# Fused attention and MLP block on one core: the second score matmul of a slot moved in between the value matmuls

## The chip, the cores and the metric

One core of a Trainium2 chip. The metric is the time on the device in microseconds (us). The kernel before takes 1401.2 us (median of 3 runs, 1400.7 to 1401.65).

Names in the profile: PE is TensorE's matmuls, PEld its weight loads, ACT is ScalarE, DVE VectorE, POOL GpSimd. `f_S` is the score buffer in PSUM, `f_PQ` holds q and the exponentials, `f_KV` holds K and V, `f_O` the attention output in PSUM, `f_M` the PSUM buffer of the projections.

## The reference

```python
def _A_ref(x, k_cache, v_cache, wq, wo):             # x 1x2048x640, 32 heads, 2048 keys, head size 128
    q = (x @ wq)...                                  # heads split off
    scores = einsum('bhqd,bhkd->bhqk', q, k_cache) * Dh ** -0.5
    p = _softmax(scores); o = einsum('bhqk,bhkd->bhqd', p, v_cache)
    return o... @ wo
# around it: modulation from c, layernorm, residual; then _B_ref: layernorm, GELU, shifts, w2, layernorm, w3, GELU, w4
```

All in bf16. About 1190 of the 1400 us are attention, the rest is the MLP part (called the tail here).

## The kernel before

The program lists operations with priorities; a planner then fixes each engine's order. On PE the order is simply by priority. Attention runs in 128 steps (8 groups of 4 heads x 4 chunks of 512 queries x the head in the group), each of 8 slots, one per pair of key tiles. In a slot PE computes two 512-column score matmuls into one of two score buffers (`S0`, `S1`, used in turn), and ACT takes the exponential of the whole buffer, 128x1024. The value matmuls of a key tile (four of 129 columns: two for each of two output buffers) follow about three slots later. Query projection (`q_proj`) and output projection (`wo_group`) fill in.

```python
S_ps = [ps("S%d" % i, [128, 1024]) for i in range(2)]        # the two score buffers
PV_SLOTS = [2, 2, 3, 2, 2, 3, 2]                             # key tiles' value matmuls per slot
...
for j in range(NP):                                          # NP = 8 slots in step s
    n = s * NP + j
    sp = Tile(pool="S%d" % (n % 2))
    pt = PT[n % NPT]
    for r in range(2):
        kt = 2 * j + r
        P.op("PE", lambda e, ...: e.matmul(sp[:, r * QC:(r + 1) * QC], K_ap[b][:, kt * 128:(kt + 1) * 128], q.ap, start=True, stop=True),
             MM(QC), (K[b][kt // 4], q), (sp,), n + 0.01 * r, accum=True)            # last number: priority
    x = P.op("ACT", lambda e, ...: e.activation(pt.ap..., sp.ap, ACT.Exp, scale=SCALE), 1021, (sp,), (pt,), n)
    for r in range(2):
        u = 2 * j + r
        ...                                                  # slot, acc from PV_SLOTS
        key = NP * s + 3 + slot + 0.3 + 0.01 * (u - acc)
        for bk in range(2):
            kb = key + 0.004 * bk if u < NKT - 2 else NP * s + 9.35 + 0.02 * bk + 0.001 * u
            P.op("PE", pv, 2 * MM(129), (pt, V[b]), (o[bk],), kb, accum=True)        # pv: two matmuls
# q_proj of the next step: priority NP * s + 2.3 + ...; output projection: about n + 0.6
```

Two facts follow from the code. A slot's first score matmul can't start before the exp of two slots earlier has read the buffer. And that exp can't start before the second score matmul of its own slot is done.

## Time and profile before

The page of the profiled run. After the bar of a group line come busy time, mean ns of one instruction, then the idle time of the engine before the group and what ended it.

```profile
span 1395.0 us, 29964 instructions
...
PE 1380.7 (99%) x13176; PEld 939.8 (67%) x13176; DVE 518.0 (37%) x1337; ACT 1114.6 (80%) x1195; POOL 123.5 (9%) x106
...
PE 96%; ACT 2%; POOL 1%; DVE 0%; DMA 0%; issue 0%; ACTq 0%; POOLq 0%
...
L714 ACT ACTIVATE f_PQ<-f_S 128x1024 bf16<-128x1024 f32 x1024 | 1030.2, 1023 | 155.0 <-PE f_S L712 147.6
...
L731 PE MATMUL f_O<-f_KV,f_PQ 128*128 128x129 bf16 x8192 | 612.2, 220 | 0.2 <-ACT f_PQ L714 0.2
L712 PE MATMUL f_S<-f_PQ,f_KV 128*128 128x512 bf16 x2048 | 608.9, 379 | 3.1 <-ACT f_PQ L714 2.7
```

PE is nearly the whole chain of waits; exp waits for scores (147.6 us in all), scores hardly for exp (2.7 us). But 99% busy doesn't say how near to its limit PE is, since matmuls overlap in the records. That is read from the starts. One slot in the PE timeline (columns: start us, us, engine, line, operation, tiles, count):

```profile
701.80 0.59 PE L712 MATMUL f_S<-f_PQ,f_KV 128*128 128x512 bf16 x2
702.23 0.62 PE L731 MATMUL f_O<-f_KV,f_PQ 128*128 128x129 bf16 x8
702.68 0.30 PE L668 MATMUL f_M<-f_wo,f_OO 128*128 128x320 bf16 x1
702.82 0.59 PE L712 MATMUL f_S<-f_PQ,f_KV 128*128 128x512 bf16 x2
```

Two scores take 0.43 us, eight value matmuls 0.45 us (56 ns each), one output projection 0.14 us: a slot of 1.02 us. Taken one by one, the start-to-start gaps are 216 ns for 512 columns, 136 for 320: each is the columns divided by 2.4 GHz plus about 2.5 ns. I call that the floor. From the first to the last score matmul, everything above it sums to 9.28 us; in steps 9 to 118, to 4.59 us of some 1026 us (42 ns a step).

Then the slack. This is the timeline ahead of a slot with twelve value matmuls (slot 5), ACT, PEld and PE together:

```profile
699.13 2.05 ACT L714 ACTIVATE f_PQ<-f_S 128x1024 bf16<-128x1024 f32 x2 [0.73 <-PE f_S L712]
...
700.41 0.23 PEld L712 LDWEIGHTS f_S<-f_PQ,f_KV 128*128 128x128 bf16 x2
700.55 0.38 PE L712 MATMUL f_S<-f_PQ,f_KV 128*128 128x512 bf16 x1
```

The first of the two exps ends at 699.13 + 1.02 = 700.15; the score matmul that reuses its buffer starts at 700.55, about 0.39 us later, and its weight load at 700.41. The exp is done in good time. Slots are counted from 0; slots 0 and 5, both with twelve value matmuls, have the least slack (388 ns by the median of steps 9 to 119), since the two slots ahead of each are the shortest pairs, 1.02 us each.

### The profile page before, as it was taken

Reading aid. Unit: us, or ns where it says so; the run is one execution under the profiler, and the core shown is the slowest. Engines: PE = TensorE matmul, PEld = TensorE weight load, DVE = VectorE, ACT = ScalarE, POOL = GpSimd, SP = SyncE. Lnnn points to the kernel's source line nnn. Section 1 sums busy time; section 2 is a strip of 40 time slices with the busy share of each in tenths; the row PEclk is TensorE's granted clock in tenths of the full one; section 3 lists DMA queues with packets and bytes.
Section 4 is the critical chain, followed back from the end, with each engine's and each line's share of the span. In section 5 each row is a group of like instructions: output and inputs, shape, how many; then the busy total and the mean of one; then the engine's idle time right before and its main releaser. Section 6 shows DMA issues by size and latency. Waiting matters only on the chain.

```text
span 1395.0 us, 29964 instructions
## 1 busy us (share of the span) xinstructions
PE 1380.7 (99%) x13176; PEld 939.8 (67%) x13176; DVE 518.0 (37%) x1337; ACT 1114.6 (80%) x1195; POOL 123.5 (9%) x106
## 2 busy tenths in 40 slices
PE   8999999999999999999999999999999999899998
PEld 6666676766676667666776677666766766555554
DVE  4453333233323332333223332333233345595552
ACT  5988888888888888888888888888888888864222
POOL 0000000000000000000000000001233376600000
PEclk9999999999999999999999999999999999999999
DMA  9551623261214221241215112612254112411110
GB/s 203 126 110 34 134 61 85 51 107 35 47 35 88 55 47 35 55 88 33 49 22 98 33 40 33 107 35 47 54 103 102 17 31 55 111 39 48 34 39 24
DMA packets 258963, 88.82 MB, mean 64 GB/s; under 512 B 236625, under 2 KB 257554, under 8 KB 258834
## 3 DMA queue, kind: packets, MB, share of 16 engines
q1 hardware_dynamic: 256210, 85.41, 30.1%
q8 instruction: 104, 1.70, 0.5%
q10 hardware_dynamic: 2624, 1.51, 0.5%
q14 instruction: 25, 0.20, 0.1%
HBM read 43.48 MB, written 2.62 MB: 33 GB/s over the span
## 4 chain that ended last, share of the span: by engine, by line
PE 96%; ACT 2%; POOL 1%; DVE 0%; DMA 0%; issue 0%; ACTq 0%; POOLq 0%
PE f_O L731 33%; PE f_S L712 31%; PE f_M L643 10%; PE f_M L668 10%; PE f_S L890 2%; PE f_M L890 2%; PE f_S L877 2%; PE f_O L877 2%; ACT f_PQ L836 1%; PE f_S L413 1%; PE f_S L850 1%; PE f_M L850 1%; POOL f_y L511 0%; PE f_S L832 0%; PE f_M L623 0%; DMA f_xin<-in_A_x_dram 0%
## 5 line engine op out<-in xcount | busy, mean ns | idle before, releaser
L714 ACT ACTIVATE f_PQ<-f_S 128x1024 bf16<-128x1024 f32 x1024 | 1030.2, 1023 | 155.0 <-PE f_S L712 147.6
L731 PEld LDWEIGHTS f_O<-f_KV,f_PQ 128*128 128x128 bf16 x8192 | 539.6, 98 | 211.4 <-ACT f_PQ L714 0.4
L731 PE MATMUL f_O<-f_KV,f_PQ 128*128 128x129 bf16 x8192 | 612.2, 220 | 0.2 <-ACT f_PQ L714 0.2
L712 PE MATMUL f_S<-f_PQ,f_KV 128*128 128x512 bf16 x2048 | 608.9, 379 | 3.1 <-ACT f_PQ L714 2.7
L676 DVE TENSOR_TENSOR f_y<-f_M,f_y 128x320 f32<-128x320 f32 x192 | 94.4, 492 | 524.8 <-PE f_M L668 524.8
L668 PE MATMUL f_M<-f_wo,f_OO 128*128 128x320 bf16 x992 | 270.2, 299 | 0.0
L712 PEld LDWEIGHTS f_S<-f_PQ,f_KV 128*128 128x128 bf16 x2048 | 192.0, 98 | 46.6 <-ACT f_PQ L714 3.9
L643 PE MATMUL f_M<-f_hT,f_wq 128*128 128x512 bf16 x640 | 159.2, 379 | 0.1
L511 POOL TENSOR_TENSOR f_y<-f_y,f_mod 128x640 f32<-128x640 f32 x40 | 61.3, 1542 | 1058.2 <-DVE f_y L676 1050.8
L668 PEld LDWEIGHTS f_M<-f_wo,f_OO 128*128 128x128 bf16 x992 | 94.9, 97 | 27.9
L643 PEld LDWEIGHTS f_M<-f_hT,f_wq 128*128 128x128 bf16 x640 | 62.4, 98 | 75.9 <-DVE f_hT L557 0.9
L740 DVE TENSOR_TENSOR f_OO<-f_O,f_rl 128x256 bf16<-128x256 f32 x256 | 108.4, 423 | 8.3
L646 DVE CAST f_PQ<-f_M 128x512 bf16<-128x512 f32 x128 | 88.5, 691 | 54.8 <-PE f_M L643 54.7
L738 DVE RECIPROCAL f_rl<-f_O 128x2 f32<-128x2 f32 x256 | 43.5, 170 | 45.9 <-PE f_O L731 41.7
L880 ACT ACTIVATE f_OO<-f_O 128x512 bf16<-128x512 f32 (+1 forms) x28 | 16.7, 596 | 33.2 <-PE f_O L877 33.1
L880 ACT ACTIVATE f_OO<-f_S 128x512 bf16<-128x512 f32 (+1 forms) x28 | 16.6, 595 | 30.7 <-PE f_S L877 30.7
L674 DVE COPY f_y<-f_M 128x320 f32<-128x320 f32 x32 | 15.7, 490 | 67.5 <-PE f_M L668 67.5
L890 PE MATMUL f_S<-f_KV,f_OO 128*128 128x320 bf16 x224 | 34.3, 300 | 0.0
L890 PE MATMUL f_M<-f_KV,f_OO 128*128 128x320 bf16 x224 | 34.3, 300 | 0.0
L472 DVE BATCH_NORM_STATS2 f_small<-f_y 128x6 f32<-128x320 f32 x64 | 29.3, 478 | 10.7 <-POOL f_y L511 10.7
L890 PEld LDWEIGHTS f_M<-f_KV,f_OO 128*128 128x128 bf16 x224 | 20.6, 97 | 14.0 <-issue 5.5
L890 PEld LDWEIGHTS f_S<-f_KV,f_OO 128*128 128x128 bf16 x224 | 20.5, 97 | 13.3 <-issue 4.2
(119 smaller groups left out, 512.5 us busy)
## 6 DMA issues: line engine op xcount, KB each, us to landing
f_KV<-in_A_v_cache_dram SPq DMA_DIRECT2D x31, 512.0 KB, 4.7
f_wo<-in_A_wo_dram SPq DMA_DIRECT2D x8, 640.0 KB, 4.3
f_xin<-in_A_x_dram SPq DMA_DIRECT2D x15, 320.0 KB, 4.1
f_wq<-in_A_wq_dram SPq DMA_DIRECT2D x7, 640.0 KB, 4.6
f_W<-in_w_mod_dram SPq DMA_DIRECT2D x4, 800.0 KB, 4.9
out_dram<-f_xin SPq DMA_DIRECT2D x16, 160.0 KB, 1.8
f_KV<-in_B_w_dram SPq DMA_DIRECT2D x5, 432.0 KB, 3.6
f_KV<-in_A_k_cache_dram SPq DMA_TRANSPOSE x128, 2.8
```

Of the source, the lines that this page charges most:

```text
L511: P.op(eng, lambda e: e.tensor_tensor(out=out, in0=a, in1=b, op=op), COST[eng][0], rd, wr, prio, lat=300 if eng == "POOL" else None)
L643: P.op("PE", lambda e, i=i, kk=kk: e.matmul(m.ap, wq_t[g % 2][:, kk, hh * 128:(hh + 1) * 128], hT_t[ch][:, kk, :], start=(i == 0), stop=(i ...
L646: P.op("DVE", lambda e: e.tensor_copy(q.ap, m.ap), 690, (m,), (q,), s * NP - 90)
L668: P.op("PE", lambda e, m=m, qt=qt, hf=hf, hh=hh: e.matmul(m[:, 0:HD], OT_ap[gs][:, qt, hh, :], wo_t[g % 2][:, hh, hf * HD:(hf + 1) * HD], ...
L676: P.op("DVE", lambda e, m=m, yt=yt: e.tensor_tensor(out=yt.ap, in0=m[:, 0:HD], in1=yt.ap, op=ALU.add), 490, (m, yt), (yt,), s * NP - 60)
L712: P.op("PE", lambda e, sp=sp, r=r, kt=kt: e.matmul(sp[:, r * QC:(r + 1) * QC], K_ap[b][:, kt * 128:(kt + 1) * 128], q.ap, start=True, stop ...
L714: x = P.op("ACT", lambda e, sp=sp, pt=pt: e.activation(pt.ap.rearrange("p k q -> p (k q)"), sp.ap, ACT.Exp, scale=SCALE), 1021, (sp,), (pt ...
L731: ins = e.matmul(o[bk][:, w * 129:w * 129 + 129], pt[:, r, qt * 128:(qt + 1) * 128], V_ap[b][:, u, 0:129], start=(u == 0 and w == 0), stop ...
L738: P.op("DVE", lambda e, ov=ov, i0=i0: e.reciprocal(rl_t[:, i0:i0 + 2].unsqueeze(2), ov[:, 0:258].rearrange("p (u d) -> p u d", u=2)[:, :, ...
L740: evac.append(P.op("DVE", lambda e, ov=ov, i0=i0, bk=bk: e.tensor_tensor(out=On_ap[gs][:, 2 * bk:2 * bk + 2, hh, :], in0=ov[:, 0:258].rear ...
L877: P.op("PE", lambda e, m=m, f=f, kk=kk, fs=fs: e.matmul(m[0:fs, :], w3_ap[:, kk, f * 128:f * 128 + fs], nT_ap[ch][:, kk, :], start=(kk == ...
L890: P.op("PE", lambda e, f=f, hf=hf, fs=fs: e.matmul(m[:, hf * 512:hf * 512 + HD], gT_ap[0:fs, f, i * 128:(i + 1) * 128], w4_ap[f][0:fs, hf ...
```

## The change

My reading of the intent: to spread the two long score matmuls of a slot among the short value matmuls, so that PE has a long matmul more often under which to load weights, and ACT gets its input more evenly.

```diff
-                     MM(QC), (K[b][kt // 4], q), (sp,), n + 0.01 * r, accum=True)
+                     MM(QC), (K[b][kt // 4], q), (sp,), n + (0.307 if 9 <= s < 120 else 0.01) * r, accum=True)
```

In the built program the second score matmul of seven slots in eight follows four value matmuls (the third slot: one query-projection matmul); in the second slot nothing lies between 0.01 and 0.307, so the pair stays together. The planner also puts some work of ACT, DVE and POOL from step 117 on in another order.

## The prediction

> **What bounds the kernel.** TensorE. The page gives PE 99% busy, ACT 80%; the chain that ended last is 96% PE. Busy is not peak, so I took starts of consecutive matmuls in the trace. From the first to the last score matmul (1187.6 of 1395.0 us) each gap is the columns at 2.4 GHz plus about 2.5 ns: 216 ns for the 512-column score matmul, 136 for 320 columns, 56 to 57 for the 129-column value matmul. The Trainium skill, "TensorE: Matmul & The Clock Gate", Back-to-back issue gap, gives N/2.4 + 2.5 ns for an isolated gap and about 81 ns sustained at N=128 with weight loads; here value matmuls with their loads hold 56.4 ns: the loads are already hidden. Everything above that floor sums to 9.3 us, only 4.6 us in the steps the change touches (9 to 119), mostly 0 to 5 ns between value matmuls; no PE gap there exceeds its floor by 25 ns. There is little to win.
>
> **What the change does.** Same instructions. In seven of eight slots of those steps the second score matmul comes after four value matmuls (in the third slot after one query-projection matmul); in the second slot the pair stays together. Each slot keeps its PE work: 432 + 8 x 56.4 + 136 = about 1020 ns, 1245 ns with twelve value matmuls. The exp (1023 ns, starting 415 ns after the second score matmul's start) comes 4 x 56.4 = 226 ns later.
>
> **Is the delay free?** Two score buffers: slot n's first score matmul needs the exp of n-2. Shortest two-slot distance: 2 x 1020 = 2040 ns; before, 216 + 415 + 1023 = 1654 ns of it used. Measured from exp's end to the next score matmul's start: 388 ns (slots 0 and 5), over 480 elsewhere. After (estimate from these): 162 ns in slots 0 and 5, 250 or more elsewhere. The weight load then starts 51 to 63 ns after exp's end instead of 254. In steps 1 to 4, which have no output-projection matmuls, that slack is already 117 ns, the load is held to 63 ns, and the PE gap shows no excess (-1 to 1 ns). So 162 ns should cost nothing. ACT's shortest start-to-start is about 920 ns, so ACT does not become the bound.
>
> **Gain.** The split falls where the 5 ns step between two key tiles' value matmuls lay: estimate 1.5 ns x 6 slots x 111 steps = 1 us. The scheduler also reorders ACT, DVE and POOL from step 117 on. In the timeline the tail's first GELU table load waits 1.17 us for a POOL memset behind a POOL chain that a small ACT group started; that group moves one exp earlier, perhaps 1 us gained. Other tail moves: plus or minus 2 us.
>
> **Time.** 1401.2 to about 1399.5 us; range 1397 to 1403. Faster by over 2%: 1%; within: 97%; slower: 2%.
>
> **What will show it.** Busy times by group unchanged; ACT 80%; a step still 9.26 us; exp end to next score start near 160 ns in slots 0 and 5; the first score matmul's weight load waiting for ACT more often, PE itself not.
>
> **What would make it wrong.** If a held weight load stalls PE by x ns, 222 slots cost 0.22x us: 50 ns would be 11 us. If alternating score and value matmuls opens gaps, six splits x 111 steps add 0.67 us per ns. If reordered small ACT work waits for DVE, the tail grows by some us.

## The result, and the profile after

1400.53 us (median of 4 runs, 1400.4 to 1400.77) against 1401.14 us (four runs): ratio 0.9996, 95% interval 0.9978 to 1.0013. The measured times can't tell the change from zero.

The page after:

```profile
span 1394.5 us, 29726 instructions
...
PE 1367.3 (98%) x12941; PEld 943.8 (68%) x13176; DVE 518.6 (37%) x1337; ACT 1125.9 (81%) x1195; POOL 123.8 (9%) x106
...
PE 96%; ACT 2%; issue 1%; DVE 0%; DMA 0%; POOL 0%; ACTq 0%; POOLq 0%
...
L714 ACT ACTIVATE f_PQ<-f_S 128x1024 bf16<-128x1024 f32 x1024 | 1041.5, 1024 | 143.5 <-PE f_S L712 106.4
...
L731 PE MATMUL f_O<-f_KV,f_PQ 128*128 128x129 bf16 x8192 | 720.2, 220 | 7.8 <-ACT f_PQ L714 0.3
L712 PE MATMUL f_S<-f_PQ,f_KV 128*128 128x512 bf16 x1856 | 671.3, 379 | 5.3 <-ACT f_PQ L714 2.2
```

Three lines invite wrong readings. PE has 12941 records and not 13176: 235 matmul records, 192 of them of score matmuls, are missing from this trace (all 13176 weight loads are there), so PE's busy time didn't really fall. The busy time of the value matmuls rose from 612 to 720 us and that of the scores from 609 to 671 us although each still takes 220 and 379 ns: busy time of a group is the union of overlapping records, and groups cut into smaller pieces overlap less with themselves. The Trainium skill, "Perfetto Trace Analysis", Identifying the Most-Contended Engine, says that matmul busy time doesn't measure the distance to the limit; this pair of traces is an example. ACT's 11 us more is the same effect: before, one exp a step overlapped its predecessor by 0.10 us, and 0.10 x 111 is 11 us.

The PE timeline, the end of one slot of eight value matmuls and one of twelve:

```profile
702.33 0.38 PE L712 MATMUL f_S<-f_PQ,f_KV 128*128 128x512 bf16 x1
702.55 0.39 PE L731 MATMUL f_O<-f_KV,f_PQ 128*128 128x129 bf16 x4
702.78 0.30 PE L668 MATMUL f_M<-f_wo,f_OO 128*128 128x320 bf16 x1
702.91 0.38 PE L712 MATMUL f_S<-f_PQ,f_KV 128*128 128x512 bf16 x1
703.13 0.39 PE L731 MATMUL f_O<-f_KV,f_PQ 128*128 128x129 bf16 x4
703.35 0.38 PE L712 MATMUL f_S<-f_PQ,f_KV 128*128 128x512 bf16 x1
703.57 0.62 PE L731 MATMUL f_O<-f_KV,f_PQ 128*128 128x129 bf16 x8
```

Every piece takes what it took before: 0.22 us a score matmul, 56 ns a value matmul. Now ahead of the slot with twelve value matmuls:

```profile
701.73 2.04 ACT L714 ACTIVATE f_PQ<-f_S 128x1024 bf16<-128x1024 f32 x2 [0.23 <-PE f_S L712]
...
702.80 0.10 PEld L712 LDWEIGHTS f_S<-f_PQ,f_KV 128*128 128x128 bf16 x1
702.91 0.38 PE L712 MATMUL f_S<-f_PQ,f_KV 128*128 128x512 bf16 x1
```

The exp ends at 702.75, the weight load follows 51 ns later (it is now held until then), and the score matmul starts at exp's end plus 159 ns, with no gap behind the matmul before it.

Where the 0.55 us between the two spans (1395.01 and 1394.46 us) lie, from the starts in the two traces (missing records filled in by the floor, from the weight loads):

| stretch | before | after | difference |
|---|---|---|---|
| start to step 9 (not changed by the edit) | 96.47 | 96.01 | -0.46 |
| steps 9 to 118, above the floor | 4.59 | 3.78 | -0.81 |
| step 119, above the floor | 0.04 | 0.51 | +0.46 |
| step 120 to the last score matmul | 72.99 | 72.90 | -0.09 |
| last score matmul to the end | 190.97 | 191.30 | +0.34 |

The first row is not the change's: in the traces of kernels that, like these two, leave steps 0 to 8 alone, step 9 starts anywhere from 96.0 to 96.9 us.

### The profile page after: what moved, and what is told of

Its sections match the earlier page's. It is cut to its first block, busy times and chain, and to the rows that moved or that the text cites. A ratio compares the mean times of both kernels' runs of the same rounds, so it can differ in the third digit from the quotient of the medians.

```text
span 1394.5 us, 29726 instructions
## 1 busy us (share of the span) xinstructions
PE 1367.3 (98%) x12941; PEld 943.8 (68%) x13176; DVE 518.6 (37%) x1337; ACT 1125.9 (81%) x1195; POOL 123.8 (9%) x106
## 4 chain that ended last, share of the span: by engine, by line
PE 96%; ACT 2%; issue 1%; DVE 0%; DMA 0%; POOL 0%; ACTq 0%; POOLq 0%
PE f_O L731 34%; PE f_S L712 29%; PE f_M L643 10%; PE f_M L668 10%; PE f_S L890 2%; PE f_M L890 2%; PE f_S L877 2%; PE f_O L877 2%; ACT f_PQ L714 1%; PE f_S L850 1%; PE f_M L850 1%; PE f_S L413 1%; PE f_S L832 1%; ACT f_PQ L836 1%; PE f_O L832 0%
## 5 line engine op out<-in xcount | busy, mean ns | idle before, releaser
L714 ACT ACTIVATE f_PQ<-f_S 128x1024 bf16<-128x1024 f32 x1024 | 1041.5, 1024 | 143.5 <-PE f_S L712 106.4
L731 PEld LDWEIGHTS f_O<-f_KV,f_PQ 128*128 128x128 bf16 x8192 | 593.7, 98 | 231.9 <-ACT f_PQ L714 0.5
L731 PE MATMUL f_O<-f_KV,f_PQ 128*128 128x129 bf16 x8192 | 720.2, 220 | 7.8 <-ACT f_PQ L714 0.3
L712 PE MATMUL f_S<-f_PQ,f_KV 128*128 128x512 bf16 x1856 | 671.3, 379 | 5.3 <-ACT f_PQ L714 2.2
L712 PEld LDWEIGHTS f_S<-f_PQ,f_KV 128*128 128x128 bf16 x2048 | 196.2, 97 | 34.4 <-ACT f_PQ L714 3.9
L643 PE MATMUL f_M<-f_hT,f_wq 128*128 128x512 bf16 x608 | 170.8, 379 | 2.2 <-DVE f_hT L557 0.5
```

The costliest lines, as they stand in the source:

```text
L643: P.op("PE", lambda e, i=i, kk=kk: e.matmul(m.ap, wq_t[g % 2][:, kk, hh * 128:(hh + 1) * 128], hT_t[ch][:, kk, :], start=(i == 0), stop=(i ...
L712: P.op("PE", lambda e, sp=sp, r=r, kt=kt: e.matmul(sp[:, r * QC:(r + 1) * QC], K_ap[b][:, kt * 128:(kt + 1) * 128], q.ap, start=True, stop ...
L714: x = P.op("ACT", lambda e, sp=sp, pt=pt: e.activation(pt.ap.rearrange("p k q -> p (k q)"), sp.ap, ACT.Exp, scale=SCALE), 1021, (sp,), (pt ...
L731: ins = e.matmul(o[bk][:, w * 129:w * 129 + 129], pt[:, r, qt * 128:(qt + 1) * 128], V_ap[b][:, u, 0:129], start=(u == 0 and w == 0), stop ...
```

## The experiments

Theory: PE is at its floor in every step the change touches, so order can save only the little above the floor; moving the second score matmul by d ns delays exp by d, which is free until the slack from exp's end to the next score matmul in that buffer is used up. Rivals: the order of score and value matmuls on PE has a price or a gain of its own through its weight loads; ACT bounds together with PE; the tail's new order makes the time.

"Above the floor" is the sum for steps 9 to 118 from each trace; before has 4.59 us.

| run | edit | time us | ratio to before, 95% | above the floor us |
|---|---|---|---|---|
| e2_late8 | split by 8 value matmuls | 1431.05 | 1.0217 [1.0200, 1.0234] | 34.25 |
| e3_pair8 | both after 8 value matmuls | 1401.07 | 1.0001 [0.9984, 1.0017] | 4.15 |
| e4_late8_halfexp | e2_late8, exp halved | 1398.63 | 0.9986 [0.9969, 1.0003] | 4.20 |
| e6_before_halfexp | before, exp halved | 1399.63 | 0.9993 [0.9976, 1.0010] | 4.58 |
| e7_late6 | split by 6 value matmuls | 1405.07 | 1.0032 [1.0016, 1.0047] | 8.14 |
| e1_pe_only | the change, PE's order alone | 1399.76 | 1.0002 [0.9988, 1.0015] | 3.78 |
| e8_to_118 | split in steps 5 to 118 | 1399.63 | 0.9995 [0.9982, 1.0009] | 3.77 |
| e5_all_steps | split in all steps | 1398.69 | 0.9988 [0.9975, 1.0002] | 3.77 |
| e9_to_118_gate | e8_to_118, tail's order fixed | 1397.39 | 0.9975 [0.9962, 0.9987] | 3.77 |
| e10_before_gate | before, tail's order fixed | 1397.67 | 0.9973 [0.9960, 0.9986] | 4.59 |

The first call's runs of before had a median of 1401.01 us, the second's 1400.49, the third's 1400.94. The record marks every result as correct, but the two halved-exp kernels leave out half of the exponentials; for them that mark can't be taken at its word.

### e2_late8, e3_pair8: is it the delay or the order?

```diff
e2_late8:   n + (0.317 if 9 <= s < 120 else 0.01) * r
e3_pair8:   n + ((0.315 + 0.002 * r) if 9 <= s < 120 else 0.01 * r)
```

> Second score matmul after eight value matmuls (451 ns later) in steps 9 to 119. Theory (buffer loop: the first score matmul of slot n needs the exp of n-2; the split is free until the slack from exp's end to that matmul, 388 ns in slots 0 and 5 before, falls under about 55 ns): natural slack 388 - 451 = -63 ns, so about 118 ns stall in slots 0 and 5 and about 20 ns in slot 2, 258 ns a step x 110 = 28 us, plus 1 to 2 us in step 119: 1427 to 1433 us. Rival (the order of score and value matmuls on TensorE matters by itself, by its weight loads; the distance of the two score matmuls doesn't): fewer alternations than the change on trial, so within 2 us of before, 1399 to 1403 us.

> Both score matmuls after the eight value matmuls, side by side; the second lies where it lies in e2_late8. Theory (only the distance from the first score matmul to exp counts): slack 388 ns as before, 1400 to 1402 us, no stalls. Rival (what costs in e2_late8 is that the second score matmul and exp come late in the slot): as slow as e2_late8, about 1430 us.

e2_late8 took 1431 us, inside the theory's range and far outside the rival's; e3_pair8, with the second score matmul in the same place among the value matmuls, took the time of before. So what costs isn't the late place in the slot but the distance between the two score matmuls of a buffer. In the e2_late8 trace (page, waits, and the timeline at a slot of twelve value matmuls):

```profile
L712 PEld LDWEIGHTS f_S<-f_PQ,f_KV 128*128 128x128 bf16 x2048 | 195.5, 97 | 141.0 <-ACT f_PQ L714 79.7
```

```profile
PEld f_S L712 <- ACT f_PQ L714: 79.7, 215, 1.4
```

```profile
700.67 2.05 ACT L714 ACTIVATE f_PQ<-f_S 128x1024 bf16<-128x1024 f32 x2 [0.22 <-PE f_S L712]
...
701.50 0.30 PE L668 MATMUL f_M<-f_wo,f_OO 128*128 128x320 bf16 x1
701.75 0.10 PEld L712 LDWEIGHTS f_S<-f_PQ,f_KV 128*128 128x128 bf16 x1 [0.37 <-ACT f_PQ L714]
701.75 0.39 PE L712 MATMUL f_S<-f_PQ,f_KV 128*128 128x512 bf16 x1
```

Exp ends at 700.67 + 1.02 = 701.70, the load starts at 701.75, and this time PE was empty: its last matmul started at 701.50 and needed 0.136 us, so PE lost about 0.12 us, the 118 ns expected. Summed: (34.25 - 4.59) us / 110 = 270 ns a step, where 258 were expected. One loose end: in e3_pair8 steps 119 and 120 lost 0.96 and 0.18 us, which I had not expected. The trace shows single gaps of 168 to 319 ns there, at score and at value matmuls; the 168 ns are the loop again (slot 1 has 160 ns of slack in the other steps, and step 119 is short of two output projections of 136 ns: 160 - 272 is 112 too little, plus the 55 ns of a held load), the others stay open.

### e4_late8_halfexp, e6_before_halfexp: is exp the thing waited for, and does ACT bound?

```diff
-            x = P.op("ACT", ... e.activation(pt.ap.rearrange("p k q -> p (k q)"), sp.ap, ACT.Exp, scale=SCALE),
+            x = P.op("ACT", ... e.activation(pt.ap[:, 0, :], sp.ap[:, 0:QC], ACT.Exp, scale=SCALE),
-                            ins = e.matmul(..., pt[:, r, qt * 128:(qt + 1) * 128], ...
+                            ins = e.matmul(..., pt[:, 0, qt * 128:(qt + 1) * 128], ...
```

> e2_late8 with exp on 512 of the 1024 columns (wrong result on purpose; same waits, about 430 ns shorter by the 512-column GELU of the tail, 595 ns against 1023). Theory (buffer loop): the slack in slots 0 and 5 becomes about -63 + 428 = 365 ns, the stalls vanish: 1397 to 1402 us, as e6_before_halfexp within 1.5 us. Rival (TensorE order): as e2_late8.

> The kernel before with exp on 512 of the 1024 columns (wrong result on purpose). Theory (TensorE at its issue floor, ACT off the path between steps 9 and 119): a step stays 9.26 us; only the start and the last steps, where ACT holds TensorE, gain: 1396 to 1401 us. Rival (ACT at 80% bounds together with TensorE): ACT loses some 430 us of work and the time falls by over 1%, under 1387 us.

Exp fell from 1023 to 597 ns. With that e2_late8's 30 us vanished (34.25 to 4.20 us above the floor; slack in slots 0 and 5 361 ns, 365 expected). Before with half the exp work took 1.4 us less, which the times can't tell from zero (interval up to 1.0010); its trace is 1.8 us shorter, 0.7 of it ahead of step 9, 0.3 from step 120 on and 0.8 after the last score matmul, while steps 9 to 118 were the same to 0.01 us. So exp's end is what e2_late8 waits for, and ACT doesn't bound the middle of this kernel: it is busy for 87% of steps 9 to 118 (888.67 of 1026.42 us), and taking away 420 us of its work in all changed nothing there.

### e7_late6: where the free room ends

```diff
e7_late6:   n + (0.312 if 9 <= s < 120 else 0.01) * r
```

> Second score matmul after six value matmuls (338 ns later), steps 9 to 119. Theory: natural slack 388 - 338 = 50 ns in slots 0 and 5, just under the 55 ns that a held load with idle TensorE shows, so about 5 ns x 222 = 1 us plus 0.8 us in step 119: 1401 to 1403 us. If instead 117 ns are needed (the shortest slack seen with no stall before), 67 ns x 222 = 15 us: 1414 to 1417 us.

1405.07 us, 2 to 4 us more than expected. Step 119 lost 0.78 us, as expected. The rest is the steps 9 to 118: (8.14 - 3.78) us / 220 slots = 20 ns a slot and not 5. The trace shows three parts: 6.7 ns before the held score matmul; 9.4 ns in the gap between it and the first value matmul (e2_late8 loses the same 9.4 ns there); and some 4 ns that have nothing to do with the hold: cut into six and two, the value matmuls of slots 3, 4, 5 and 7 keep a 4.6 ns gap that four and four takes away (next section). Why the gap after a held score matmul is longer, no run here shows. The limit itself is where the theory had it, near 55 ns after exp's end and not at 117.

| delay d, ns | slack left in slots 0 and 5: 388 - d | measured | above the floor, ns a step |
|---|---|---|---|
| 0 (before) | 388 | 388 | 42 |
| 226 (the change) | 162 | 159 | 34 |
| 338 (e7_late6) | 50 | 55, held | 74 |
| 451 (e2_late8) | -63 | 55, held | 311 |

### e1_pe_only, e8_to_118: the gain alone

e1_pe_only plans as before and then moves the matmuls in PE's list (cut):

```diff
+    def move_seconds(self):
+        pe = self.seq["PE"]
+        for o in self.moves:                       # second score matmuls, steps 9 to 118, not slot 1
+            i = pe.index(o)
+            n = 1 if o.prio % 8 > 1.9 and o.prio % 8 < 2.1 else 2
+            pe[i:i + n + 1] = pe[i + 1:i + n + 1] + [o]
...
             plan.schedule()
+            plan.move_seconds()
e8_to_118:  n + (0.307 if 5 <= s < 119 else 0.01) * r
```

> The change on TensorE alone: the program is scheduled as before, then the second score matmuls of steps 9 to 118 are moved; ACT, DVE, POOL and the DMA queue keep the order of before, the tail too. Theory (the split takes about 8 ns a step out of the gaps between value matmuls, 42 to 34 ns above the floor, and costs nothing else; step 119, which loses 0.46 us in the change, is left out): 110 x 8 ns = 0.9 us under before, about 1400.2 us, slot slacks of 160 ns as in the change. Rival (the time moved by the reordered tail): same as before within 0.2 us, 1401.1 us.

> The split as in the change, but in steps 5 to 118, all of which have output-projection matmuls. Theory: step 119's 0.46 us is won back, four more steps win 8 ns each: about 0.5 us under the change, 1400.0 us (1399.3 to 1400.7), if the tail's new order costs no more than in the change. Rival (step 119 costs nothing that the last steps don't make up): as the change, 1400.5 us.

The medians, 1399.76 and 1399.63 us, lie 0.7 and 0.9 us under before, but before itself wandered from 1399.44 to 1401.44 us in those rounds, and one of e1_pe_only's five runs took 1402.93: the times don't decide. The traces do. In both, steps 9 to 118 stand at 3.78 and 3.77 us above the floor, step 119 back at 0.04 us, and the slack in slots 0 and 5 at 159 to 160 ns. So the gain, 0.81 us, is PE's order alone, and the loss in step 119 comes only when that step is split too. Where the 8 ns a step come from shows in the gaps: after a score matmul, value matmuls run at 0.4 ns above the floor, but in a run of eight one later gap is usually 4.6 ns; cut into four and four that gap is gone in slots 3, 4 and 7 (5.2 to 3.3 ns a slot), and one of the two in slot 5 goes as well. That makes some 1.9 ns in four slots, where the prediction had 1.5 ns in six.

### e5_all_steps: a miss, and what it uncovered

```diff
e5_all_steps:   n + 0.307 * r
```

> The split in all steps 0 to 127. Theory (buffer loop): steps without output-projection matmuls (1 to 4, 120, 123, 124, 127) have 117 ns of slack, 226 ns is too much, each loses about what step 119 loses in the change (0.46 us): 8 x 0.46 = 3.7 us over the change, about 1404 us (1402.5 to 1405.5). Rival (the split is free everywhere): 1400 to 1401 us.

Both forecasts missed: 1398.69 us, the lowest time so far of a kernel that does all the work (its interval still reaches 1.0002, so it isn't clear of before). Yet the steps did lose: steps 1 to 4 went from 0.51 to 1.63 us above the floor, steps 119 to 127 from 1.02 to 2.79 us. The last score matmul started 2.26 us later than before, and the whole ended 1.0 us earlier, so the tail was 3.3 us shorter (187.7 against 190.97 us). The ACT timeline of the tail of before shows what can be saved there:

```profile
1206.92 1.28 ACT L836 ACT_TABLE_LOAD   x1 [1.17 <-POOL f_PQ L825]
1208.21 1.07 ACT L836 ACTIVATE f_PQ<-f_S 128x512 bf16<-128x512 f32 x2
1209.28 1.28 ACT L477 ACT_TABLE_LOAD   x1
...
1210.89 1.28 ACT L478 ACT_TABLE_LOAD   x1
...
1212.41 1.28 ACT L836 ACT_TABLE_LOAD   x1
1213.70 1.20 ACT L836 ACTIVATE f_PQ<-f_S 32x512 bf16<-32x512 f32 x2
```

After two GELUs (L836) ACT turns to a small group for a normalisation (L477 logarithm, L501, L478 exponential) and back, which costs three table loads of 1.28 us. PE needs those GELUs to free its PSUM buffers; its timeline, and the stretch from 1210 to 1220 us (PE, PEld, DVE, ACT, POOL busy, then the granted clock):

```profile
1210.58 1.24 PE L832 MATMUL f_O<-f_wq,f_W 128*128 128x512 bf16 x5
1215.04 0.75 PE L668 MATMUL f_S<-f_wo,f_OO 128*128 128x320 bf16 x4 [3.22 <-ACT f_PQ L836]
1216.18 1.25 PE L668 MATMUL f_O<-f_wo,f_OO 128*128 128x320 bf16 x4 [0.38 <-ACT f_PQ L836]
```

```profile
1210.00:1220.00 10.00, 6.40 (x32) 3.24 (x31) 3.87 (x9) 9.07 (x14) 4.76 (x4) 0.83 0.59 121
```

PE waits 3.22 us, and then the clock granted is lower: the gaps of ten 320-column matmuls from 1216.2 to 1218.6 us are up to 131 ns over the floor of 136, that is half speed, 1.3 us in all. The Trainium skill, "TensorE: Matmul & The Clock Gate", The HAM clock gate, says that PE drops to 1.2 GHz after an idle window of about 3.4 us. This trace is near that: 3.22 us idle, and from 1215.56 us on a granted clock of 0.5 for 3.41 us. But in e2_late8 and e4_late8_halfexp PE waited 3.24 and 3.31 us at the same place and the clock stayed at 1.00, so a wait of this length brings the drop in some traces only. The tail of e2_late8, with the wait but without the drop, took 189.75 us: estimated from this, the drop costs about 1.2 us. In e5_all_steps the planner happened to put the small group ahead of the first GELU.

### e9_to_118_gate, e10_before_gate: the tail's order on purpose

```diff
                 rstd_act(g, a, a + 2, prio, 1200.0)
+                small_act.append(P.ops[-1])
...
-                    us_ap[...], m[p0:p1, :], GELU), act(QC), (m,), (us[ch],), key)
+                    us_ap[...], m[p0:p1, :], GELU), act(QC), (m,), (us[ch],), key, after=(small_act[9], small_act[10]) if ch == 0 else ())
```

> e8_to_118 with one order added: the first GELU of the tail comes after the small ACT group (logarithm, copy, exponential for the normalisation) that otherwise runs between the first GELUs and brings three table loads of 1.28 us. e5_all_steps got this order by chance. Theory (e5_all_steps is fastest because of its tail alone): TensorE's wait in the tail falls from 3.2 to about 1.3 us, the stretch of 13 output-projection matmuls at half clock (131 ns longer each, 1.5 us) goes; with the split's 0.9 us less: about 1396.5 us (1395.5 to 1398.0). Rival (the gain of e5_all_steps comes from the split in steps without output-projection matmuls): as e8_to_118, 1399.6 us.

> The kernel before with only the tail's order added, no score matmul moved. Theory: about 3.3 us under before by the tail alone, 0.9 us over e9_to_118_gate: 1397.3 us (1396.3 to 1398.8). Rival: as before, 1400.5 to 1401.2 us.

Both fall: 1397.39 and 1397.67 us, the only versions whose interval excludes 1 on the fast side (about 0.25%). e10_before_gate, ACT, PE and the same stretch:

```profile
1207.29 0.20 ACT L477 ACTIVATE f_small<-f_small 128x2 f32<-128x2 f32 x1 [1.80 <-DVE f_small L473]
...
1207.75 1.28 ACT L839 ACT_TABLE_LOAD   x1
1209.04 2.28 ACT L839 ACTIVATE f_PQ<-f_S 128x512 bf16<-128x512 f32 x4
1211.34 2.42 ACT L839 ACTIVATE f_PQ<-f_O 64x512 bf16<-64x512 f32 x4
```

```profile
1212.81 0.70 PE L668 MATMUL f_S<-f_wo,f_OO 128*128 128x320 bf16 x4 [1.25 <-DMA f_OO<-f_OO]
```

```profile
1210.00:1220.00 10.00, 8.12 (x54) 4.85 (x52) 6.11 (x15) 6.43 (x12) 4.42 (x4) 1.00 0.62 114
```

ACT waits 1.80 us for the group's input, saves the three loads, PE waits 1.25 us, now for the transposing DMA, and the clock stays at 1.00. From the last score matmul to the end: 187.9 us, against 190.97. The split adds to this 0.82 us of the trace in steps 9 to 118 (4.59 to 3.77), too little for these rounds to show in the times: the two kernels are equal within their spread.

## Why the prediction was right

- **The bound.** Right. PE stood at its floor (value matmuls at 56.9 ns on average, where the prediction has 56.4); halving exp left the middle steps the same (4.58 against 4.59 us).
- **The delay is free.** Right, with its numbers: 226 ns later predicted and 226 found (the second score matmul starts 442 ns after the first and not 216), 162 ns of slack against 159, no stall. e2_late8 and e7_late6 show what lies beyond, e3_pair8 and e4_late8_halfexp that it is this loop. One reading in it was off: the weight load 63 ns after exp's end in steps 1 to 4 wasn't held. It starts 54 ns ahead of its matmul, as loads behind a value matmul do in e3_pair8 with 615 ns of slack; a held one starts 51 ns after exp's end. The conclusion doesn't hang on it, since 117 ns of slack without a PE gap was measured.
- **The gain.** 1 us from the gaps; measured 0.81 us. But the prediction missed step 119, which lies in the range and has no output-projection matmuls to fill its slots: in slot 5 its slack is 117 ns, 226 are taken, and the score matmul came 168 ns late (226 - 117 + 55 is 164). Another 294 ns were lost ahead of the first score matmul of step 120; 0.14 us of that is a small ACT group (L477, L501, L478) that the planner moved ahead of the exp waited for. Together that is the 0.46 us, of which 0.09 us come back in step 120, where the group had delayed the exps before. The prediction named this very slack, for steps 1 to 4, and did not look whether such a step lay in the range. In the trace after, that step's waits include:

```profile
PEld f_S L712 <- ACT f_PQ L714: 0.5, 2, 0.3
```

- **The tail.** "Perhaps 1 us gained" did not happen. The POOL memset came 0.88 us earlier (1205.82 against 1206.70), but only because everything did: it starts 2.66 us after the last score matmul in both traces, and in e1_pe_only, whose tail isn't reordered. The small ACT group that the prediction had in mind did move one exp earlier, and POOL's work with it, by 1.15 us; but the next such group moved one exp later, and POOL (before, then after) waited for it:

```profile
1205.04 1.75 POOL L519 TENSOR_SCALAR f_y<-f_hT,f_small 128x640 f32<-128x640 bf16 x2
1206.70 0.14 POOL L825 MEMSET f_PQ<- 128x20 bf16 x1
```

```profile
1204.14 1.74 POOL L519 TENSOR_SCALAR f_y<-f_hT,f_small 128x640 f32<-128x640 bf16 x2 [1.00 <-ACT f_small L478]
1205.82 0.12 POOL L825 MEMSET f_PQ<- 128x20 bf16 x1
```

The wait for the GELUs remained (3.25 us), and the tail from the last score matmul on grew by 0.34 us. Nearly all of that is the half-clock stretch (explained under e5_all_steps): its slow gaps sum to 1.36 us in the trace before and 1.68 in the trace after. In e1_pe_only, with the tail's order of before, they sum to 1.23 us and the tail is 190.51 us, so this difference isn't shown to be the change's. The predicted 1399.5 us was 1.0 us low, well within its range. That the kernel stays within 2% follows from the bound and the slack alone; the parts about the tail were wrong and too small to matter.
- **What would show it.** Two signs were badly chosen. Busy times by group did not stay the same, because they are unions of overlapping records. And the held weight load hardly shows as a wait (3.9 us in both profiles, in 3 and 5 waits), because it starts while other work fills PE; it shows only in its start, 51 ns after exp's end.

So the gain that the edit seems meant for didn't get lost: it was never there. Weight loads were hidden before, and with PE starting its matmuls every N/2.4 + 2.5 ns, a new order could win no more than the 4.59 us above that in steps 9 to 118; it won 0.81.

## What to carry to other kernels

Before reordering matmuls, compare the starts of consecutive matmuls with columns / 2.4 GHz + 2.5 ns; if they agree, order can win no more than what lies above that sum, and it can lose far more (30 us in e2_late8). A split between the first writer of a buffer and the last one spends the slack of the loop through that buffer, so work out the slack where slots are shortest, and look at the steps that lack the filler work. When an edit moves a planner's other decisions, read the stretches that the edit did not touch: here the only gain that the times show (0.25%) lay in the tail, in a wait behind three table loads and the clock drop that may follow it.

## What the Trainium skill lacked or had wrong

- "TensorE: Matmul & The Clock Gate", Back-to-back issue gap: about 81 ns per matmul sustained at N=128 with a weight load each. Here 8192 matmuls of 129 columns, each with its load, ran at 56.9 ns on average (in steps 9 to 118), and 512-column ones at 216 ns and not at about 131: the formula that the page calls isolated is the one that holds.
- I found no page with a figure for how late a weight load may come. Here a load held until 108 ns before its matmul was free; when PE had run dry the matmul started 4 ns after its load, 55 ns after exp's end, and 9.4 ns more were lost in the gap after it.
- "ScalarE: Activation LUTs", What ACT_TABLE_LOAD costs: 1283 ns for the load agrees (1.28 us), but its further 1380 ns of drain per switch is not seen in the tail: loads begin as the activation before them ends (1209.28 us) and the next activation starts as they end.
- "Perfetto Trace Analysis" warns of matmul busy time, but I found nothing in it on missing matmul records (235 of 13176 in one trace, none in another) or on group busy times that grow by 18% (612 to 720 us) when the same matmuls are only interleaved.
